# Last four chunks: the second product by seven block products too, with block sums staged in DRAM, seven open accumulators and one bank for the first product

## The chip, the cores and the metric

The kernel runs on one core of one Trainium2 chip. The time is the device time of the whole program in microseconds (us); lower is better. A difference under 2% counts here as no change.

## The reference, cut to what matters

The input is attention without softmax (8 batches, 8 heads, 576 tokens, 64 dims, 128 random features), and its output feeds a feed-forward layer with a squared relu:

```
def phi(x):
    proj = np.einsum('bhsd,df->bhsf', x, w_phi)
    proj = proj - np.max(np.abs(proj), axis=-1, keepdims=True)
    return np.concatenate([np.exp(proj), np.exp(-proj)], axis=-1)
...
num = np.einsum('bhsf,bhfd->bhsd', q_p, kv)
den = np.einsum('bhsf,bhf->bhs', q_p, z)[..., None] + 1e-06
...
h = x @ w_in                 # x is [4608, 512], w_in [512, 2048]
r = np.maximum(h, 0.0)
return (r * r) @ w_out       # w_out is [2048, 512]
```

## The kernel before

**Tiles.** The 4608 tokens of the feed-forward layer are 18 chunks of 256 tokens, d_ff is 8 blocks of 256 columns. One turn is one block of d_ff for one chunk or, late in the program, for a pair of chunks. The first product makes h for the turn in PSUM (the accumulator memory of eight banks), ACT and DVE square it and split it into a high part `gh` (f32r) and a low part `gl` (bf16), and the second product adds the turn's share to an output accumulator that stays open over all 8 turns.

**Precision by passes.** The first product takes each matmul three times in fp16 (high times high, high times low, low times high). The second takes it three times too: bf16 upper part times low weights, bf16 `gl` times rounded weights, and f32r `gh` times high weights. So 12 matmuls of 512 columns make the second product of one chunk and turn (`gemm2`, L1088).

**Chunks 1 to 10 and the pairs.** Ten chunks run with the plain first product (L1051, 24 matmuls of 256 columns) beside the attention work. The last eight chunks run as four pairs: (13,14), (15,16), (17,10), (11,12). After three plain turns at its start, `pair` (L1190) takes the first product of two chunks as one block product of 2 by 2 blocks with seven products instead of eight (L1233): 7 x 6 = 42 matmuls of 256 columns per turn, not 48. They go to three tiles: `pz` (one bank, the first product's a11 b11), `pp` (two banks, four products) and `ph` (one bank, two products). ACT copies `pz` out (L335), DVE adds the blocks together (L1248, three of 512 and one of 256 elements per partition), ACT takes relu and two squares per chunk (L1265, L1068, L1070), DVE makes `gl` (L331). Then comes `gemm2` for each chunk, with accumulators in `po` (two banks) and in `pn` and `pv`. The seven products need sums of blocks of the weights (`add_w`) and of the inputs (`add_x`), made on DVE in the stretch before; the weight sums of all eight blocks of d_ff stay in on-chip memory.

**The order.** One planner (`Plan`) lists every operation with an engine, a duration, what it needs and a rank; `improve` replaces the ranks by those of a written-out table, `RANKS`, for operations whose rank is under `MOVED`, and the resulting list is emitted. Each engine then runs its own list in that order and waits at whatever is not ready: an operation that is late holds back all that stand behind it on its engine.

**The end.** `store` (L1111) scales each finished accumulator of 128 x 512 on ACT (`o`), and a DMA writes it out.

Of the kernel before, what the change touches and what calls it, by code (L numbers as in the profile page):

```python
# [52 lines left out]
MOVED = 70.0  # L53
# [5 lines left out]
PLAIN = 3  # L59
SPILLED = (10, 11, 12)  # L60
# [257 lines left out]
def tile_kernel(ctx, tc, qp, kp, vp, w_phi, w_in, w_out, out):  # L318
# [747 lines left out]

    def squares(n, r, after, use, Q):
        sq = P.add("ACT", act_us(512), lambda: A.activation(out=gh_[n], in_=r(), func=AF.Square),  # L1068
                   after, use + [("gh", n)], Q)
        o = P.add("ACT", act_us(512), lambda: A.activation(out=r(), in_=r(), func=AF.Square),  # L1070
                  [sq], use, Q, other=[("DVE", 0.70, lambda: V.tensor_tensor(
                      out=r(), in0=r(), in1=r(), op=ALU.mult), 4.0)])
        return P.add("DVE", 0.70, lambda: sub(V, gl_[n], r(), gh_[n].bitcast(F32)),
                     [o, sq], use + [("gh", n), ("gl", n)], Q, lock=4.0)
# [51 lines left out]
    def take(use, shape, dtype, box):  # L1126
        if use not in box:
            box[use] = {"e": e_, "qe": qe_, "pt": pt_, "mx": mx_, "n": n_, "rb": rb_, "v": v_, "k": k_, "q": q_, "r": r_}[use[0]].shaped(
                use[1], shape, dtype)
        return box[use]  # L1130

    def combine(fill, sums, use, halves, after, rank):
        one, tm = ("es", NPAIR), lambda: es_[NPAIR]
        o = P.add("DVE", 1.3, fill, after + [ring1] + exps[NPAIR - 2] + in_pair.get("tm", []), [one], rank, lock=4.0)
        o = P.add("DVE", 1.7, sums, [o], [one], rank, lock=4.0)
        hi = P.add("ACT", 1.06, lambda: A.activation(out=halves(0), in_=tm(), func=AF.Copy), [o], [one] + use, rank,
                   other=[("DVE", 0.64, lambda: V.tensor_copy(out=halves(0), in_=tm()), 4.0)])
        o = P.add("DVE", 1.28, lambda: sub(V, halves(1), tm(), halves(0)), [hi], [one] + use, rank, lock=4.0)
        in_pair["tm"] = [o]
        return o  # L1140

    def add_w(f, rank):
        use = {0: [("e", 64)], 1: [("e", 65)], 2: [("e", 66)], 3: [("pt", 32)], 4: [("rb", 32), ("rb", 33)], 5: [("mx", 64), ("n", 32)],
               6: [("qe", 66)], 7: [("v", 36), ("r", PAIRED * NFP + 2 * PLAIN)]}[f]
        box, cs = {}, slice(256 * f, 256 * f + 256)

        def halves(x):
            if len(use) == 2:
                return take(use[x], [128, 1024], F16, box)
            return take(use[0], [128, 2, 1024], F16, box)[:, x, :]  # L1150

        grid = lambda x: x.rearrange("p (h k j c) -> p h k j c", h=2, k=2, j=2)
# [12 lines left out]
        o = combine(fill, sums, use, halves, w_done[f, True], rank)
        parts_w[f] = o, use, lambda x, h, k, j: grid(halves(x))[:, h, k, j, :]

    keep = {}

    def add_x(cs, rows, use, after, rank):  # L1170
# [15 lines left out]

        o = combine(fill, sums, use, halves, [o for c in cs for o in ready(c, (rows, rows + 2))] + after, rank)
        parts_x[cs, rows] = o, use, lambda x, h, i: grid(halves(x))[:, h, i, :]

    def pair(cs, pos, f, turn, po):  # L1190
        n = pos * NFP + 2 * turn
        m = TAIL + n
        Q = m - 1000.0
        g = in_pair["n"] = in_pair.get("n", -1) + 1
        px, py, pu = ("pp", ("w", g)), ("ph", BANKS + PAIRED * NFP + 2 * PLAIN + g), ("pz", ("w", g))
        grid = lambda x: x.rearrange("p (j t) -> p j t", j=2)
        X = lambda i: grid(pp_["w", g][:, i, :])
        Y = lambda: ph_[py[1]]
        rt = ("qe", 64 + g % 2)

        def r():
            if rt not in in_pair:
                in_pair[rt] = qe_.shaped(rt[1], [128, 4, T], F32)
            return in_pair[rt]

        w_ready, w_use, ws = parts_w[f]
        x_ready = [parts_x[cs, i][0] for i in range(2)]
        x_use = [y for i in range(2) for y in parts_x[cs, i][1]]
# [26 lines left out]

        def one():
# [10 lines left out]
        def plus(to, a, b):  # L1247
            V.tensor_tensor(out=to, in0=a, in1=b, op=ALU.add)  # L1248

        wide = lambda x: x.unsqueeze(1).to_broadcast([128, 2, T])  # L1250
        after = list(w_done[f, True]) + [w_ready] + x_ready + in_pair.get("pe", [])
# [4 lines left out]
        p2 = P.add("PE", 2.62, two, [p1], [px, py] + reads, m + 0.01)  # L1256
        in_pair["pe"] = [p2]
# [14 lines left out]
        in_pair["r", g] = done  # L1272

# [55 lines left out]
    free, used = [], []  # L1329
    for k, cs in enumerate(PAIRS):  # L1330
# [8 lines left out]
        for f in range(0 if k else NFP):
            add_w(f, first + 1.5 + f + 1.0 * PLAIN * (f >= NFP - PLAIN))  # L1340
        turns = [*range(NFP - PLAIN, NFP), *range(NFP - PLAIN)] if k == 0 else range(NFP)
        for j, f in enumerate(turns):
            if k or j >= PLAIN:
                pair(cs, v, f, j, po)
            else:
# [4 lines left out]
        free += [(back[c][0] if c in back else SLOT[c], used[-1]) for c in cs]  # L1350
    pool_next.after += pool_prep
# [32 lines left out]
    "L=6CLUTFEO2uPvAD.-.-Ht3`E*LhX{c?L|81TPLM/%B1.CGQn<cD>of`k:Rv35E9p?e$W-WMWIrtOQ1OhEaM9p48lUaroXtSqqwO"  # L1384
    "Qfxx]kEayQn*WdMJ<h=X/Aar|tOBKo0@Nm|e2{=}sZn4q[G={R:AyMy.YirRbF0EF-0jB5/.@uD%JIZbseAlhb.07:d{2-W6Lj=M"
    "IaPC7fA-P|nhy;|gK+UB[M?$mr3#3pJ<Tim?[ygPhFUO^Yz<9]Dq.-dw5k3{m^_H8s23LP@U:S/>N$Dm;#^ZHPVgR+xh_4v(.-ts"
# [55 lines left out]
```

## Time and profile before

| | us |
|---|---|
| runs: 1022.18 and 1020.33, median | 1021.25 |
| span of the profiled execution | 1018.5 |
| PE (TensorE, matmuls) busy | 999.8 (98%) |
| DVE (VectorE) busy | 763.2 (75%) |
| ACT (ScalarE) busy | 680.5 (67%) |
| POOL (GpSimd) busy | 361.2 (35%) |
| granted TensorE clock, mean of the span | 1.00 from 600 us on |

The profiled execution has no other time of its own than its span; the runs' times are device times with the start and end of the program, so the median is 2.75 us above the span. The last 320 us hold the pairs. The columns of each view stand at its first group below. PE rows show a matmul's time from its start to its modelled end, so that consecutive ones overlap: the pace of the engine is the distance of their starts.

### The profile page before, as it was taken

The page shows a single profiled execution, that of the slowest core. Times are in us where ns is not written, and L with a number is a line of the kernel's source. Part 1 is how long each engine was busy: PE and PEld are TensorE (multiplying, and loading weights), DVE is VectorE, ACT ScalarE, POOL GpSimd, SP SyncE. Part 2 cuts the span into 40 slices and gives each one's busy share as a digit, 9 for nine tenths or more (in the row PEclk, how much of TensorE's full clock was granted, in tenths as well). Part 3 has the DMA queues.
Part 4 walks back from the last instruction along what each step waited for, and adds up shares of the span by engine and source line. Part 5 has one row for each costly group of instructions (what it writes and reads, how often), then busy time and mean ns, then how long its engine had stood idle before and what let it go on. Part 6 is the DMA issues. An engine that isn't in the chain of part 4 may idle for free.

```text
span 1018.5 us, 19261 instructions
## 1 busy us (share of the span) xinstructions
PE 999.8 (98%) x7632; PEld 694.6 (68%) x7713; DVE 763.2 (75%) x1221; ACT 680.5 (67%) x1206; POOL 361.2 (35%) x138
## 2 busy tenths in 40 slices
PE   8999999999999999999999999999999999999998
PEld 4657776776666667666767666666776767677675
DVE  5899878798878989777879888798888447343432
ACT  6989886777777787686777867776555445435444
POOL 2433356364456555475375646563000000000000
PEclk9999999999999999999999999999999999999999
DMA  9754323132322233233324212110002001000001
GB/s 355 282 186 135 122 81 94 39 110 73 85 60 81 75 93 93 60 82 81 107 80 111 83 48 69 41 41 22 13 2 83 1 1 49 14 1 21 22 1 42
DMA packets 94914, 77.34 MB, mean 76 GB/s; under 512 B 58088, under 2 KB 72424, under 8 KB 92776
## 3 DMA queue, kind: packets, MB, share of 16 engines
q1 hardware_dynamic: 94536, 75.59, 24.6%
q8 instruction: 60, 0.98, 0.4%
q10 hardware_dynamic: 288, 0.52, 0.1%
q14 instruction: 30, 0.25, 0.1%
HBM read 61.16 MB, written 14.78 MB: 75 GB/s over the span
## 4 chain that ended last, share of the span: by engine, by line
PE 90%; DVE 3%; DMA 3%; ACT 2%; issue 1%; SPq 0%; DVEq 0%; ACTq 0%
PE po L1088 27%; PE ph L1051 21%; PE pp L1233 7%; PE pz L669 4%; PE pv L1088 4%; PE pn L1088 4%; PE ph L1233 3%; PE pn L904 3%; PE pn L884 2%; PE pp L611 2%; PE pv L904 2%; PE pz L1233 2%; PE pz L674 1%; PE pv L669 1%; PE pz L892 1%
## 5 line engine op out<-in xcount | busy, mean ns | idle before, releaser
L1051 PE MATMUL ph<-ring,win 128*128 128x256 f16 x2064 | 240.4, 273 | 0.8 <-ACT r L1060 0.8
L1051 PEld LDWEIGHTS <-win 128*128 128x128 f16 x2064 | 195.3, 98 | 47.0 <-issue 24.8
L982 POOL PARTITION_ALL_REDUCE mx<-pt x52 | 121.6, 2339 | 122.7 <-ACT pt L335 84.3
L1088 PE MATMUL po<-wh,gh 128*128 128x512 f32 x448 | 143.8, 442 | 0.0
L1003 POOL PARTITION_ALL_REDUCE rb<-rb x26 | 96.5, 3712 | 112.0 <-DVE rb L1000 95.6
L1265 ACT ACTIVATE qe<-qe,cw 128x512 f32<-128x512 f32 x58 | 41.4, 715 | 112.5 <-DVE qe L1248 112.5
L1088 PE MATMUL po<-wl,gl 128*128 128x512 bf16 x448 | 115.1, 379 | 0.0
L331 DVE TENSOR_TENSOR gl<-r,gh 128x512 bf16<-128x512 f32 x86 | 87.5, 1018 | 31.7 <-ACT r L1070 30.7
L1003 POOL PARTITION_ALL_REDUCE ds<-ds x26 | 98.7, 3797 | 25.2 <-DVE ds L1000 24.5
L1088 PE MATMUL po<-wl,gh 128*128 128x512 bf16 x375 | 101.5, 379 | 4.9 <-issue 1.6
L1088 PEld LDWEIGHTS <-gl 128*128 128x128 bf16 x576 | 56.4, 98 | 68.0
L1088 PEld LDWEIGHTS po<-wh,gh 128*128 128x128 f32 x448 | 84.6, 189 | 25.9
L1248 DVE TENSOR_TENSOR qe<-pp,qe 128x512 f32<-128x512 f32 (+1 forms) x87 | 52.3, 602 | 61.3 <-PE pp L1233 59.5
L1060 ACT ACTIVATE r<-ph,cw 128x512 f32<-128x512 f32 x86 | 58.7, 683 | 51.0 <-PE ph L1051 49.3
L331 DVE TENSOR_TENSOR gl<-qe,gh 128x512 bf16<-128x512 f32 x58 | 40.1, 691 | 65.7 <-ACT qe L1070 65.6
L1088 PEld LDWEIGHTS <-gh 128*128 128x128 bf16 x576 | 52.3, 98 | 50.7 <-issue 8.9
L633 ACT ACTIVATE e<-e 128x512 f32<-128x512 f32 x64 | 40.0, 625 | 32.3 <-DVE e L630 32.3
L1233 PEld LDWEIGHTS <-win 128*128 128x128 f16 x522 | 48.8, 98 | 14.2 <-issue 7.8
L1068 ACT ACTIVATE gh<-r 128x512 fp32r<-128x512 f32 x86 | 54.1, 629 | 5.7 <-PE pv L1088 2.0
L1070 ACT ACTIVATE r<-r 128x512 f32<-128x512 f32 x86 | 54.3, 631 | 2.7
L650 DVE TENSOR_TENSOR es<-e 128x512 f32<-128x512 f32 x52 | 46.3, 890 | 4.5 <-ACT e L635 4.3
L669 PE MATMUL pz<-e,v 128*64 128x256 f32 x416 | 49.3, 379 | 0.0
(286 smaller groups left out, 1970.4 us busy)
## 6 DMA issues: line engine op xcount, KB each, us to landing
v<-in_vp_dram SPq DMA_DIRECT2D x32, 320.0 KB, 4.1
k<-in_kp_dram SPq DMA_DIRECT2D x32, 288.0 KB, 4.1
q<-in_qp_dram SPq DMA_DIRECT2D x32, 288.0 KB, 3.4
rb<-rd SPq DMA_DIRECT2D x64, 144.0 KB, 3.1
out_dram<-o SPq DMA_DIRECT2D x34, 256.0 KB, 2.1
td<-kvs SPq DMA_DIRECT2D x26, 128.0 KB, 2.6
kz<-td SPq DMA_DIRECT2D x26, 128.0 KB, 2.9
spill<-ring SPq DMA_DIRECT2D x6, 256.0 KB, 2.9
```

Of the source, the lines that this page charges most:

```text
L331: eng.tensor_tensor(out=out_, in0=a, in1=b_, op=ALU.subtract)
L669: PE.matmul(out=to[64 * h:64 * h + 64, 0:256], lhsT=v_[p][:, t, h, :], rhs=e_[2 * p + h][:, t].rearrange("p s f -> p (s f)"), start=t == 0 ...
L904: PE.matmul(out=to[64 * h:64 * h + 64, :], lhsT=kz_[n][:, 128 * s_ + 64 * h:128 * s_ + 64 * h + 64], rhs=qe_[2 * n + h].rearrange("p (s x) ...
L982: o = P.add("POOL", par_us(S), lambda n=n, h=h: G.partition_all_reduce(mx_[n], pt_[p][:, h, :], channels=128, reduce_op=bass_isa.ReduceOp. ...
L1003: o = P.add("POOL", 3.6, lambda y=y: G.partition_all_reduce(y(), y(), channels=128, reduce_op=bass_isa.ReduceOp.add), [o], [home], R(RQ + ...
L1051: PE.matmul(out=ph[:, j, :], lhsT=win[w][:, t, 128 * ff:128 * ff + 128], rhs=at_ring(c, x, t), start=k == 0, stop=k == 3 * KT - 1)
L1060: o = P.add("ACT", act_us(512, 1), lambda: A.activation(out=r_[n], in_=ph_[bank], func=AF.Relu, scale=cw[:, f, 0:1]), [g1], [("ph", bank), ...
L1068: sq = P.add("ACT", act_us(512), lambda: A.activation(out=gh_[n], in_=r(), func=AF.Square), after, use + [("gh", n)], Q)
L1070: o = P.add("ACT", act_us(512), lambda: A.activation(out=r(), in_=r(), func=AF.Square), [sq], use, Q, other=[("DVE", 0.70, lambda: V.tenso ...
L1088: PE.matmul(out=bank(i), lhsT=x[:, j, 128 * i:128 * i + 128], rhs=w[:, j, :], start=turn + j + s == 0, stop=(turn, j, s) == (NFP - 1, 1, 2))
L1233: PE.matmul(out=to, lhsT=fl(x, *al)(k), rhs=fr(y, *ar)(k), start=n == 0, stop=n == 5)
L1248: V.tensor_tensor(out=to, in0=a, in1=b, op=ALU.add)
```

## The change

Constant `FROM` = 2: the pairs 3 and 4 (chunks 17, 10, 11, 12; 16 of the program's turns) go through a new function `blocks`. Pairs 1 and 2 keep `pair`. The first three turns of pair 1 stay plain.

- In `blocks` the first product has the same 42 matmuls, but in four pieces pa, pb, pc, pd (6, 12, 12, 12 matmuls), which all go through the one bank `ph`. Each piece is taken out by ACT (pa) or DVE (pb, pc, pd) before the next may start.
- The second product of a chunk is a product of 2 by 2 blocks too: seven products of 3 matmuls of 256 columns, 42 matmuls per turn for the two chunks instead of 24 of 512 columns. Each of the seven has an accumulator of its own (128 x 256, open over all 8 turns): both chunks' fill the seven other banks.
- New per turn: DVE makes four sums S0 to S3 of the squared blocks (both chunks in one instruction, 256 elements per partition), ACT and DVE split them into `hs` and `ls` (two instructions each, 512 elements).
- New after a pair: `collect` adds the seven accumulators of a chunk together (one ACT copy, DVE o1 to o4), ACT scales four blocks of 128 x 256, and two DMAs write them out.
- Sums of blocks of w_out (`make_t`) are made during pairs 1 and 2, stored to DRAM (1 MB per block of d_ff) and loaded again per turn. The sums of w_in (`make_w`) have two buffers now, are stored when made, and loaded again per turn (512 KB).
- `MOVED` goes from 70 to 1000: the table `RANKS` now sets the order of the whole program, and it has new contents.

```diff
-MOVED = 70.0
+MOVED = 1000.0
+FROM = 2
...
+    def blocks(cs, pos, f, turn, k, w_part, t_part):
...
+        two = lambda i, x, y: lambda: (product(bank(i)[:, 0, :], *x), product(bank(i)[:, 1, :], *y))
...
+        pa = P.add("PE", 0.66, lambda: product(bank(0)[:, 0, :], "a11", "b11"), after, [("ph", i0)] + reads, m)
+        first, other = copy(T, lambda: r()[:, 1, :], lambda: bank(0)[:, 0, :])
+        ca = P.add(*first, [pa] + old, us(0), Q - 300.0, other=[other])
+        pb = P.add("PE", 1.31, two(1, ("a12", "b21"), ("s2", "t2")), [pa], [("ph", i0 + 1)] + reads, m + 0.01)
+        cb_ = P.add("DVE", dve_us(512), lambda: plus(r()[:, 0:4:3, :], bank(1), wide(r()[:, 1, :])), [ca, pb], us(1), Q - 300.0)
+        pc = P.add("PE", 1.31, two(2, ("s3", "t3"), ("s1", "t1")), [pb], [("ph", i0 + 2)] + reads, m + 0.02)
+        cc_ = P.add("DVE", dve_us(512), lambda: plus(r()[:, 1:3, :], bank(2), wide(r()[:, 3, :])), [cb_, pc], us(2), Q - 300.0)
+        c22 = P.add("DVE", dve_us(T), lambda: plus(r()[:, 3, :], bank(2)[:, 0, :], r()[:, 2, :]), [cc_], us(2), Q - 300.0)
+        pd = P.add("PE", 1.31, two(3, ("a22", "t4"), ("s4", "b22")), [pc], [("ph", i0 + 3)] + reads, m + 0.03)
...
+        cd = P.add("DVE", dve_us(512), lambda: plus(r()[:, 1:3, :], bank(3), r()[:, 1:3, :]), [pd, c22], us(3), Q - 300.0)
...
+        for fn in (lambda E: add(E, S(0), a(1, 0), a(1, 1)), lambda E: sub(E, S(1), S(0), a(0, 0)),
+                   lambda E: sub(E, S(2), a(0, 0), a(1, 0)), lambda E: sub(E, S(3), a(0, 1), S(1))):
+            x = [P.add("DVE", dve_us(256), lambda fn=fn: fn(V), x, [rt, st], Q + 0.2, lock=4.0,
+                       other=[("POOL", pool_us(256), lambda fn=fn: fn(G), 0.0)])]
...
+            y = P.add("ACT", out_us(512), lambda hs=hs, i=i: A.activation(out=hs(), in_=s()[:, i], func=AF.Copy), after, [st] + use, Q + 0.3,
+                      other=[("DVE", 0.42, lambda hs=hs, i=i: V.tensor_copy(out=hs(), in_=s()[:, i]), 4.0)])
+            y = P.add("DVE", dve_us(512), lambda hs=hs, ls=ls, i=i: sub(V, ls(), s()[:, i], hs().bitcast(F32)), [y] + reading.get((z, 1), []), [st] + use, Q + 0.3, lock=4.0)
...
+                for s_ in range(3):
+                    for q_n, (bank_n, d), xs, ws in what:
+                        if xs[0] == "a":
+                            x = (upper(buffer(z, 0)), buffer(z, 1), buffer(z, 0))[s_][:, 2 * xs[2] + xs[1], :]
+                        else:
+                            x = (upper(hs()), ls(), hs())[s_][:, xs[1], :]
+                        if ws[0] == "b":
+                            w = (low, near, highs[f])[s_][:, ws[1], 256 * ws[2]:256 * ws[2] + 256]
+                        else:
+                            w = t_at(tb, (1, 2, 0)[s_])[:, ws[1], :]
...
+                        PE.matmul(out=to, lhsT=x, rhs=w, start=not turn and not s_ and begin,
+                                  stop=turn == NFP - 1 and s_ == 2 and q_n in ((1, 3, 5, 6) if i else (3, 5, 6)))
...
+    def collect(c, v, i, banks, Q):
...
+        o0 = P.add(*first, [told[0, 1], told[1, 1]], [rx, ry], Q, other=[other])
+        o1 = P.add("DVE", dve_us(512), lambda: plus(X(), at(0), wide(Y()[:, 0, :])), [o0, told[i, 6]], [rx, ry] + banks, Q)
+        o2 = P.add("DVE", dve_us(512), lambda: plus(Y(), at(1), wide(X()[:, 1, :])), [o1, told[i, 5]], [rx, ry] + banks, Q)
+        o3 = P.add("DVE", dve_us(256), lambda: plus(X()[:, 1, :], at(1)[:, 0, :], Y()[:, 1, :]), [o2], [rx, ry] + banks, Q)
+        o4 = P.add("DVE", dve_us(512), lambda: plus(Y(), at(2), Y()), [o3, told[i, 3]], [rx, ry] + banks, Q)
...
+            w_part = w_flow.load(f, m - 8.0) if f in w_flow.stored else w_flow.make(f, m - 8.0, make_w)
+            if k < FROM:
+                pair(cs, v, f, j, po, w_part)
+                continue
+            blocks(cs, v, f, j, k, w_part, t_flow.load(f, m - 8.0))
```

**What stands where on DVE.** Before, DVE's list for one turn of a pair has six instructions: the blocks of pp, ph and pp added (L1248), then `gl` of each chunk (L331):

```order
L1248 TENSOR_TENSOR qe_8746<-pp_10711,qe_8746 128x512 x2
L1248 TENSOR_TENSOR qe_8746<-ph_10742,qe_8746 128x512
L1248 TENSOR_TENSOR qe_8746<-pp_10711,qe_8746 128x256
L331 TENSOR_TENSOR gl_10805<-qe_8746,gh_10801 128x512
L331 TENSOR_TENSOR gl_10836<-qe_8746,gh_10832 128x512
L1248 TENSOR_TENSOR qe_8829<-pp_10788,qe_8829 128x512 x2
```

In the change, a turn of pairs 3 and 4 (squared blocks in qe_8856, the next turn's first product into qe_8770) has twelve. The tile names are reused buffers: qe_8423 holds S0 to S3, gl_10194 is the second chunk's low part, et_10231 and et_10241 are `ls` of the two chunks:

```order
L1320 TENSOR_TENSOR qe_8770<-ph_10839,qe_8770 128x2x256
L332 TENSOR_TENSOR gl_10194<-qe_8856,gh_10165 128x512
L1170 TENSOR_TENSOR qe_8423<-qe_8856 128x2x128
L332 TENSOR_TENSOR qe_8423<-qe_8423,qe_8856 128x2x128
L1320 TENSOR_TENSOR qe_8770<-ph_10866,qe_8770 128x512
L1320 TENSOR_TENSOR qe_8770<-ph_10866,qe_8770 128x256
L332 TENSOR_TENSOR qe_8423<-qe_8856 128x2x128
L332 TENSOR_TENSOR qe_8423<-qe_8856,qe_8423 128x2x128
L332 TENSOR_TENSOR et_10231<-qe_8423,ds_10227 128x512
L1320 TENSOR_TENSOR qe_8770<-ph_10903,qe_8770 128x512
L332 TENSOR_TENSOR et_10241<-qe_8423,v_10229 128x512
L332 TENSOR_TENSOR gl_10281<-qe_8770,gh_10254 128x512
```

In the order of the code's names these are cb of the next turn, gl of the second chunk, S0, S1, cc and c22 of the next turn, S2, S3, ls of the first chunk, cd of the next turn, ls of the second chunk, and then gl of the next turn's first chunk. The addition that frees the bank after pd (cd) stands behind `ls`.

**ACT in the same turn** has nine instructions: relu, square (`gh`) and square in place for each chunk, between them the copy ca of the next turn's pa (L336), and at the end `hs` of both chunks (L1467):

```order
L1437 ACTIVATE qe_8770<-qe_8770,cw 128x512
L1443 ACTIVATE gh_10254<-qe_8770 128x512
L336 ACTIVATE qe_8856<-ph_10707 128x256
L1445 ACTIVATE qe_8770<-qe_8770 128x512
L1437 ACTIVATE qe_8770<-qe_8770,cw 128x512
L1443 ACTIVATE mx_10283<-qe_8770 128x512
L1445 ACTIVATE qe_8770<-qe_8770 128x512
L1467 ACTIVATE n_10348<-qe_8423 128x512
L1467 ACTIVATE rb_10350<-qe_8423 128x512
```

Before there are seven: the same six and the copy of `pz`; `hs` is new, and the copy has gone between the squares of the first chunk.

**The end of the program on DVE.** Before, DVE's last work is the two `gl` of the last turn; the accumulators go to ACT only. In the change the last ten instructions of DVE are `ls` of both chunks and o1 to o4 of both:

```order
L332 TENSOR_TENSOR kvs_10352<-qe_8423,n_10348 128x512
L332 TENSOR_TENSOR dn_10362<-qe_8423,rb_10350 128x512
L1320 TENSOR_TENSOR r_11900<-pp_10168,r_11901 128x512
L1320 TENSOR_TENSOR r_11901<-pp_10168,r_11900 128x512
L1320 TENSOR_TENSOR r_11900<-pp_10168,r_11901 128x256
L1320 TENSOR_TENSOR r_11901<-pz_10169,r_11901 128x512
L1320 TENSOR_TENSOR r_11953<-po_11169,r_11954 128x512
L1320 TENSOR_TENSOR r_11954<-po_11170,r_11953 128x512
L1320 TENSOR_TENSOR r_11953<-po_11170,r_11954 128x256
L1320 TENSOR_TENSOR r_11954<-pn_10203,r_11954 128x512
```

Each of these four reads what the one before it wrote, and ACT's four scalings of the chunk (L1542) stand behind the last of them.

## Rows read from the trace of the kernel before

**Rows 1.** Page, span and part 1: busy us (share of span), instructions
```profile
span 1018.5 us, 19261 instructions
PE 999.8 (98%) x7632; PEld 694.6 (68%) x7713; DVE 763.2 (75%) x1221; ACT 680.5 (67%) x1206; POOL 361.2 (35%) x138
```
**Rows 2.** Windows of the pairs: busy us and (instructions) per engine, PE clock, DMA
```profile
700.00:800.00 100.00, 97.88 (x651) 69.21 (x658) 84.18 (x132) 53.38 (x82) 4.96 (x2) 1.00 0.08 25
...
900.00:1018.50 118.50, 113.93 (x738) 79.79 (x746) 43.65 (x68) 51.26 (x84) 0.00 (x0) 1.00 0.05 19
```
**Rows 3.** Timeline at PE's two longest late waits: start, us; [idle before <- releaser]
```profile
705.74 0.69 ACT L1060 ACTIVATE r<-ph,cw 128x512 f32<-128x512 f32 x1 [2.21 <-PE ph L1051]
...
706.48 0.70 PE L1051 MATMUL ph<-ring,win 128*128 128x256 f16 x5 [0.78 <-ACT r L1060]
...
781.03 0.83 PE L1233 MATMUL pp<-ring,win 128*128 128x256 f16 x6 [0.87 <-DVE qe L1248]
```
**Rows 4.** Chain that ended last, 850 to 1020: start, us, instructions
```profile
900.47 2.62 PE pp L1233 x24
...
909.74 0.67 PE pz L1233 x6
910.41 2.62 PE pp L1233 x24
913.03 1.31 PE ph L1233 x12
```
**Rows 5.** Timeline of the end: PE, then ACT's last scaling
```profile
1008.96 0.61 PE L1088 MATMUL po<-wl,gh 128*128 128x512 bf16 x2
...
1010.31 0.61 PE L1088 MATMUL po<-wl,gh 128*128 128x512 bf16 x2
...
1013.69 0.82 PE L1088 MATMUL pv<-wh,gh 128*128 128x512 f32 x2
1014.66 0.69 ACT L1111 ACTIVATE o<-pv,cc 128x512 f32<-128x512 f32 x1 [0.64 <-DMA out_dram<-o]
```
**Rows 6.** Lines by form: count | busy us, mean ns of one | idle before
```profile
L1088 PEld LDWEIGHTS po<-wh,gh 128*128 128x128 f32 x448 | 84.6, 189 | 25.9
L1088 PEld LDWEIGHTS <-gl 128*128 128x128 bf16 x576 | 56.4, 98 | 68.0
L331 DVE TENSOR_TENSOR es<-es 128x256 f32<-128x256 f32 x56 | 24.7, 442 | 1.8
L1248 DVE TENSOR_TENSOR qe<-pp,qe 128x256 f32<-128x256 f32 x29 | 12.3, 424 | 1.0
L335 ACT ACTIVATE qe<-pz 128x256 f32<-128x256 f32 x27 | 10.2, 379 | 21.3 <-PE pz L1233 21.3
L1155 DVE TENSOR_TENSOR es<-win,win 128x1024 f32<-128x1024 f16 x8 | 9.7, 1213 | 0.1
```
**Rows 7.** Timelines with f32 weight loads: two of 128 columns, then PE with sixteen
```profile
21.05 0.30 PEld L422 LDWEIGHTS pn<-ident,m 128*128 128x128 f32 x2 [0.24 <-PE pv L714]
...
308.88 1.90 PE L669 MATMUL pz<-e,v 128*64 128x256 f32 x16
310.60 0.60 PE L674 MATMUL pz<-et,v 128*64 128x256 f32 x4
```
**Rows 8.** Timelines of DVE and ACT, one turn of a pair
```profile
962.82 1.42 DVE L1248 TENSOR_TENSOR qe<-pp,qe 128x512 f32<-128x512 f32 x2 [4.02 <-PE pp L1233]
...
965.06 0.72 ACT L1265 ACTIVATE qe<-qe,cw 128x512 f32<-128x512 f32 x1 [4.55 <-DVE qe L1248]
...
966.48 0.63 ACT L1070 ACTIVATE qe<-qe 128x512 f32<-128x512 f32 x1
967.02 0.71 ACT L1265 ACTIVATE qe<-qe,cw 128x512 f32<-128x512 f32 x1
...
968.42 0.63 ACT L1070 ACTIVATE qe<-qe 128x512 f32<-128x512 f32 x1
```
**Rows 9.** Page, part 2: GB/s that the DMA engines moved, in 40 slices
```profile
GB/s 355 282 186 135 122 81 94 39 110 73 85 60 81 75 93 93 60 82 81 107 80 111 83 48 69 41 41 22 13 2 83 1 1 49 14 1 21 22 1 42
```

More of the change, by code (lines that the diff above doesn't have):

```diff
@@ L1127, in take @@
         if use not in box:
-            box[use] = {"e": e_, "qe": qe_, "pt": pt_, "mx": mx_, "n": n_, "rb": rb_, "v": v_, "k": k_, "q": q_, "r": r_}[use[0]].shaped(
+            box[use] = {"e": e_, "qe": qe_, "pt": pt_, "mx": mx_, "n": n_, "rb": rb_, "v": v_, "k": k_, "q": q_, "r": r_,
+                        "ds": ds_, "et": et_, "kz": kz_, "kvs": kvs_, "dn": dn_, "gh": gh_, "gl": gl_}[use[0]].shaped(
                 use[1], shape, dtype)
         return box[use]
[L1132 to L1140, printed above, removed]
@@ new lines, in tile_kernel, with t_at, w_put, w_get @@
+    spare_after = lambda: [o for c in range(NCH) if SLOT[c] in spare_slots for o in chunk_done.get(c, [])]
+    def t_at(b, x):
+        if not x:
+            return take(t_home(b)[0], [128, 4, 256], F32R, keep)
+        half, c0 = place(spare_slots[b % 2])
+        return ring[half][x - 1][:, :, c0:c0 + T].bitcast(BF16)
+    def w_put(f, b):
+        return 1 if f is None else SP.dma_start(ws_[f], w_at(b))
+    def w_get(f, b):
+        return 1 if f is None else SP.dma_start(w_at(b), ws_[f])
@@ L1245, in two @@
             product(Y()[:, 1, :], "s4", "b22")
[L1247 to L1251, printed above, removed]
+        after = list(w_done[f, True]) + w_ready + x_ready + in_pair.get("pe", [])
         if not turn:
@@ L1329, in tile_kernel @@
     free, used = [], []
+    in_pair["ph"] = BANKS + PAIRED * NFP + PLAIN + FROM * NFP
+    in_pair["r_at"] = PAIRED * NFP + 2 * PLAIN
+    taken_over = P.add("PE", 0.0, lambda: None, [], [], TAIL + PAIRED * NFP)
+    late_f = [*range(NFP - PLAIN, NFP)]
+    turns = [late_f + [*range(NFP - PLAIN)]] + [[*range(NFP)]] * 3
+    pool_back = P.add("POOL", 6.2, lambda: None, [op for op in P.ops if op.eng == "POOL" and op.rank > PER_PAIR * EARLY], [], -100.0)
     for k, cs in enumerate(PAIRS):
@@ L1336, in tile_kernel @@
         for i in range(2):
-            add_x(cs, i, homes[k % 2][2 * i:2 * i + 2], used[k - 2] if k > 1 else [], first + 0.5 * i)
+            add_x(cs, i, homes[k % 2][2 * i:2 * i + 2], used[k - 2] if k > 1 else list(t_flow.stored.values()) if FROM < 2 else [], first + 0.5 * i - 6.0 * min(k, 2))
+        if not k:
+            for f in range(NFP):
+                t_flow.stage(f, first + 2.0 + (2.0 * FROM - 1.0) * f, make_t)
         po = [[("po", 2 * BANKS + PAIRED + v + i) for i in range(2)], [("pn", ("o", v // 2)), ("pv", ("o", v // 2))]]
[L1339 to L1345, printed above, removed]
+        in_pair["pool"] = k + 1
+        if k == FROM:
+            in_pair["busy"] = True
+        for j, f in enumerate(turns[k]):
+            m = TAIL + v * NFP + 2 * j
+            if not k and j < PLAIN:
                 for i in range(2):
```

380 lines of the change are left out of this document (309 added, 71 removed).

## The prediction, made before the changed kernel ran

> **What bounds the kernel now.** First the page: TensorE (PE) is busy 999.8 of 1018.5 us; DVE has 25% of its time free, ACT a third [rows 1]. What PE has left is 18.7 us, so a change gains only by shortening PE's own list, and loses wherever it makes PE wait. Second, the windows of the pairs: from 900 us on PE has 113.9 of 118.5 us, the clock is granted in full (1.00), DVE works 43.7 us and ACT 51.3; but in 700:800, where the sums for the pairs are made, DVE is busy 84% [rows 2]. So pairs 3 and 4 have room on DVE and ACT, pair 1 has little. Third, the timeline where PE waits longest late in the program: 0.78 us at 706 for ACT and 0.87 us at 780 for DVE, both for an accumulator to be read out [rows 3]. The first shows what a hand-over costs: ACT's read ends at 705.74 + 0.69 = 706.43, PE starts at 706.48, 0.05 us later. Fourth, the chain of waits in the last pairs: nothing but PE, one turn per 910.41 - 900.47 = 9.94 us, of which the first product takes 0.67 + 2.62 + 1.31 = 4.60 us (24 matmuls of 256 columns in 2.62, so 0.109 each), and the second product the other 5.34 us [rows 4].
>
> All sums below are against the span of 1018.5 us; the median of the runs, 1021.25, is 2.75 us above it, and I add that at the end.
>
> **The change part by part.**
>
> *Fewer columns on PE.* The second product of a turn goes from 24 matmuls of 512 columns to 42 of 256: 48 x 0.109 = 5.23 us becomes 42 x 0.109 = 4.58 us of streaming. The 5.34 measured is 0.11 above its streaming, and the turn has 8 f32 matmuls: 0.014 us for each. At the end six matmuls of 512, two of them f32, take 1010.31 - 1008.96 = 1.35, which is 0.04 above 12 x 0.109: 0.02 for each f32 one [rows 5]. The new list has 14 products of three matmuls, with one f32 each: 3 x 0.109 + 0.02 to 0.03 = 0.35 to 0.36; I take 0.36. Turn: 4.60 + 14 x 0.36 = 9.64, against 9.94. Sixteen turns: **-4.8 us**. The lower bound of a product is 0.327 (no extra), a turn of 9.18, -12.2 us. The upper bound is in the weights: one f32 load shows 189 ns, a 16-bit one 98 [rows 6]; a load of 189 behind a matmul of 109 would add 0.08 per product, 0.44 in all, a turn of 10.76. Against it: two such loads together take 0.30 us, so that the second starts 0.11 after the first, and sixteen f32 matmuls of 256 columns, each with a load, go by in (310.60 - 308.88)/16 = 0.108 each [rows 7]. That is the nearest row and the reason for 0.36.
>
> *The new loop through one bank.* Before, the first product has three tiles and waits for none of them in these turns. Now each piece must be read out of `ph` before the next starts. From the end of a last matmul's stream to the end of its record goes 0.16 us (five matmuls show 0.70, of which 5 x 0.109 stream [rows 3]), and I take the hand-over of 0.05 to the reader and back. With ACT's 379 ns [rows 6] that is 0.64 us after pa; with DVE's 0.69 (two in 1.42 [rows 8]) 0.95 after pb and pd, and with c22's 424 ns [rows 6] behind it 1.4 after pc. The usual order of PE has three, three, five and three products between the pieces (1.08, 1.08, 1.80, 1.08 us), so the bank by itself is covered. What is not is DVE's place: cd, which frees the bank after pd, stands behind `ls`, and `ls` hangs on a loop: cd 0.69; ACT's six instructions 3.99 (965.06 to 968.42 + 0.63 [rows 8]) and the copy ca 0.3 between them; gl 0.69; S0, S1 0.88 (442 ns each [rows 6]); cc and c22 1.11; S2, S3 0.88; hs 0.68; ls 0.69; some 0.15 for the hand-overs. That is 10.1 us. Neighbours that don't depend on each other overlap (ACT's 966.48 + 0.63 ends 0.09 after the next began at 967.02 [rows 8]); four such places on DVE take it to 9.75. I take 9.9: PE waits 0.26 us per turn in the 14 middle turns, **+3.6 us**. Bounds: 0 where the loop is under PE's 9.64, and 0.76 x 14 = 10.6 where DVE or ACT slips to 10.4 (some turns have only one or two products between two pieces, each missing one 0.36).
>
> *Entry.* In the first two turns of pair 3 there are no second products to put between pieces: pa and pb, pd and pa, and again pa and pb stand side by side, 0.64 + 0.95 + 0.64 = 2.2 us. The first S products then need the whole loop once: from cd some 10 us, and PE has 8.3 us of work there: 1.4 more, after overlap. **+3.6 us** (2.2 to 5).
>
> *Pair boundary and end.* Between pairs 3 and 4 `collect` puts 2 x (3 x 0.69 + 0.42) = 5.0 us on DVE, and the new pair's first products wait for the banks it reads; PE has the first product of the new pair meanwhile: **+2.5 us** (1 to 5). In the last turn no first product is left to cover the loop; from the last piece 9 us of cd, ACT, gl, S, hs and ls stand before the last S products, about as long as the products that are left, so I take **+1.2 us** (0 to 3). After the last matmul there was one ACT scaling of 0.69 [rows 5]; now there are what is left of o2, o3, o4 (1.9 us after overlap) and four scalings of 256, about 1.6: **+2.7 us** (2 to 3.7).
>
> *Sums and transfers in pairs 1 and 2.* The sums of w_out cost DVE 1.2 (1213 ns [rows 6]) + 4 x 0.44 + about 1.2 for the low part, 4.2 us each, 34 in all, into 16 turns whose DVE is 84% busy at the start and under half later: **+1 us** (0 to 4). The loads are 1.5 MB per turn, 159 GB/s; the DMA engines moved 355 in the first slice and under 50 in most of the last ten [rows 9], and two buffers give them a turn's lead: 0. They stand on SP's queue, where little else is left but the outputs. If a load were late, PE would stop at the first product that uses it.
>
> *The order of the whole.* In the new order eight other matmuls stand between the two tiles that made PE wait at 706, and ten at 780: **-1.65 us** [rows 3]. The order of the first 600 us changes little; 0.
>
> Sum: -4.8 + 3.6 + 3.6 + 2.5 + 1.2 + 2.7 + 1.0 - 1.65 = +8.15. Span 1026.7, **1029 us** as a median of runs.
>
> **The rivals.**
> - *The loop is covered and products are cheap: faster.* If products take 0.336 (0.009 extra, under the 0.014 of the long ones) a turn is 9.30 and the gain 10.2; with entry 3, middle 1, boundary 1.5, end 0.5 + 2.7, sums 0 and -1.65 the sum is -3.2: 1018; with the middle at 0 and entry 2.2, 1016. It needs DVE's loop to come down by 0.6 us per turn. For it: DVE and ACT are under half busy there [rows 2]. Against it: the loop is a chain, and idle time in it is waiting for its own links. Range 1010 to 1021; chance 0.22.
> - *DVE's list slips: slower, within 2%.* Turn 10.4, +10.6 in place of +3.6: 1036 (1034 to 1041). It decides where the middle turns show PE waiting for cd more than 0.5 us. Chance 0.14.
> - *f32 weights bound the short matmuls: slower.* Each f32 load, now behind a matmul of 256 columns and not of 512, takes its 189 ns: a product 0.44, a turn 10.76, 13.1 us lost in place of 4.8 gained. DVE's loop is then hidden (-3.6 of it): +8.15 + 17.9 - 3.6 = +22.5, 1044. It decides from 0.02 us above the 0.36 of a product (0.38 costs what the columns save). For it: 189 against 98 [rows 6]; against it: the loads 0.11 apart [rows 7]. Chance 0.07.
>
> On this rival, the Trainium skill ("TensorE: Matmul & The Clock Gate", section "Weight-path perf modes — Fast Weight Load (FWL) and DoubleRow") says that the fast load is given to 128 weights of any type but FP32: it speaks against a change that loads f32 weights twice as often per column, and 189 against 98 agrees [rows 6]. The same page's "LDWEIGHTS (loading the stationary operand)" reckons a load by its columns over 1.2, an estimate of 107 ns for 128: by that it just hides behind 109, a turn stays 9.64 and the rival falls; the 0.11 between two loads agrees with this one [rows 7].
>
> **How the numbers follow.** The forecast of 1029 (its own range 1021 to 1036, from the bounds of the loop, the entry and the boundary) has a chance of 0.55; the three rivals 0.22, 0.14 and 0.07; 0.02 is left for what I have not seen. Signs are mixed, so the range takes in most of the faster rival and most of the slip: 1011 to 1040 leaves out a tenth of the forecast and of these two, and the weights. More than 2% (20 us, about what a measurement of this kernel can tell from no change) is 1000.8 or 1041.7: faster could come only from the lower bound of every term, 0.01; slower is the weights and the end of the slip, 0.09; the rest, 0.90, is within.
>
> **What would show it.** In the trace after: the starts of pa in pairs 3 and 4 9.9 us apart, with PE idle 0.2 to 0.4 us a turn before pa, released by DVE's addition from `ph`, and nearly none before pb, pc and pd; three-matmul products 0.36 apart; the last matmul about 4 us before the last scaling ends; no waits of 0.8 us at the start of pair 1. Products of 0.38 or more would make the weights right; a turn under 9.7 without waits the faster rival; idle time before pb or pc a slip. Waits for a DMA on PE, or a granted clock under 1.00, would be neither forecast nor rival.

## The result, and the profile after

The changed kernel takes **1031.88 us** (median of 1030.05 and 1033.7) against 1021.25: a ratio of 1.0103 (95% interval 1.0056 to 1.0151), a small loss, within the 2% taken as no change. The forecast was 1029, range 1011 to 1040. Run again beside the experiments the change took 1033.88 against 1020.57, 1.0124 (1.0099 to 1.0148). One execution of a later run, the profiled one of `square_dve2`, went at a granted clock of 0.655 and took 1469 us; nothing below is read from it.

The profiled execution's span went from 1018.5 to 1031.9 us, by 13.4 us, while the medians are 10.6 apart. The runs on record that have both times take 1.8 us more than their span (1033.7 against 1031.9). So the profiled execution of the change is the slower of its two, that of the kernel before (1018.5, hence 1020.33) the faster, and of the 2.75 us between span and median in the prediction about 1 is scatter. Where the two traces part is read from the first matmul of each stage:

| stage | before | after | difference |
|---|---|---|---|
| to the first product of pair 1 | 722.39 | 726.00 | +3.61 |
| pairs 1 and 2 | 127.57 | 126.79 | -0.78 |
| pair 3 to the last turn of pair 4 | 149.06 | 149.38 | +0.32 |
| last turn to the end of the last matmul | 15.49 | 20.86 | +5.37 |
| from there to the end | 4.02 | 8.89 | +4.87 |

The third and fourth rows do not hold the same work. When the last turn begins, the change still has 36 second products to do, eight more than the 28 of two turns; eight are 2.8 us. For the same work the third row is about +3.2 and the fourth +2.5.

The page after (its span and part 1) and the windows of the pairs; they answer to [rows 1, 2]:

```profile
span 1031.9 us, 20283 instructions
...
PE 1004.3 (97%) x8002; PEld 717.5 (70%) x8002; DVE 823.3 (80%) x1383; ACT 710.8 (69%) x1262; POOL 359.9 (35%) x140
```

```profile
700.00:800.00 100.00, 100.00 (x689) 71.73 (x689) 91.30 (x143) 63.59 (x96) 4.98 (x2) 1.00 0.39 130
...
900.00:1031.90 131.90, 117.52 (x1012) 100.99 (x1009) 87.39 (x163) 70.66 (x128) 0.73 (x1) 0.98 0.47 152
```

DVE is fuller in pair 1 (91%) and PE still has no idle time there: the sums are hidden. From 900 us on DVE's work has doubled and PE leaves 14 us unused, 9 of them at the end; the granted clock of 0.98 is theirs too (0.73 from 1024 to 1031, where no matmul runs). PE's busy time is no measure of the columns saved: the page before lacks some matmul records (7632 of 7713 loads), this one none.

PE's waits (engine, line, releaser: us in all, times, longest):

```profile
PE ph L1314 <- DVE qe L1320: 3.8, 7, 0.9
...
PE ph L1314 <- ACT qe L336: 1.4, 3, 0.5
...
PE pp L1489 <- DVE r L1320: 0.8, 1, 0.8
...
PE pp L1489 <- DVE et L332: 0.6, 1, 0.6
...
PE pz L1489 <- DMA e<-ws: 0.3, 1, 0.3
```

The one bank's hand-overs lead (ph): all ten stand at the entry of pair 3, at the boundary of the pairs and in the last three turns. The last row names a load, but that matmul, at 867.50, reads `gl`, which DVE had finished at 867.44 (its row: start 866.75, 0.69 us). So none of the new loads is shown to make PE wait. These rows hold only what PE's modelled ends don't cover. A middle turn shows more. The chain of waits through one, from pc (898.02) to pa (903.76):

```profile
898.02 1.34 PE ph L1314 x12
...
899.39 0.70 DVE qe L1320
...
900.11 0.42 DVE qe L1320
...
900.54 0.68 DVE qe L332 x2
...
901.24 0.64 ACT n L1467
...
901.90 0.70 DVE kvs L332
...
902.65 1.11 PE pp L1489 x8
903.76 0.67 PE ph L1314 x6
```

pc, then cc, c22, S2 and S3, `hs`, `ls`, and then eight matmuls of the products behind pd. On PE's timeline the same place:

```profile
902.27 0.27 PE L1489 MATMUL pp<-ring,n 128*128 128x256 bf16 x1
902.65 0.28 PE L1489 MATMUL pp<-ring,kvs 128*128 128x256 bf16 x1
902.69 0.36 PE L1489 MATMUL pp<-pt,n 128*128 128x256 f32 x1
...
903.61 0.83 PE L1314 MATMUL ph<-ring,win 128*128 128x256 f16 x6
```

The product's second matmul takes `ls` (kvs) and starts 0.38 us after the first, not 0.11: a wait of 0.27 us inside the product, of which the bars leave only 0.11 open, since the first bar lasts 0.27. So in this loop I took waits as the distance of starts less the matmuls' own time. That gives 4.2 us at the entry of pair 3, 1.3 in the middle turns, 2.4 at the boundary of the pairs, 1.8 before two pieces of the last three turns and 2.3 behind the last piece. Products themselves take 0.355 us, and a turn without waits 9.55 (turn 4 of pair 3).

The 1.3 us of the middle turns are three waits of 0.28 for `ls` (turns 5, 7 and 8 of pair 3) and two of 0.24 and 0.25 for the bank (turn 6 of pair 3, turn 1 of pair 4), where only two products stand between pb and pc. The turns 4, 5 and 7 of pair 4 have no wait at all. There PE's list runs the second products three to six products (1.1 to 2.1 us) further behind the pieces of the first product than in pair 3, so that `ls` is in time; that this is the reason is argued from the lists, and no run tests it.

Two of the bank's waits, at the entry and at the boundary, then two waits of the last turn, for the bank and for `ls` (et):

```profile
854.09 0.82 PE L1314 MATMUL ph<-ring,win 128*128 128x256 f16 x6 [0.47 <-ACT qe L336]
...
952.02 0.81 PE L1314 MATMUL ph<-ring,win 128*128 128x256 f16 x6 [0.89 <-DVE qe L1320]
...
1009.35 0.50 PE L1314 MATMUL ph<-k,win 128*128 128x256 f16 x3 [0.91 <-DVE qe L1320]
...
1012.22 0.28 PE L1489 MATMUL pp<-ring,et 128*128 128x256 bf16 x1 [0.57 <-DVE et L332]
```

And the end, which answers to [rows 5]; the last matmul ends at 1023.03:

```profile
1020.76 0.27 PE L1489 MATMUL pp<-ring,n 128*128 128x256 bf16 x1 [0.78 <-DVE r L1320]
...
1023.27 1.30 ACT L1542 ACTIVATE o<-r,cc 128x256 f32<-128x256 f32 x3 [2.02 <-DVE r L1320]
...
1024.48 0.36 ACT L336 ACTIVATE r<-pv 128x256 f32<-128x256 f32 x1
1024.88 1.94 DVE L1320 TENSOR_TENSOR r<-po,r 128x512 f32<-128x512 f32 x3 [1.64 <-ACT r L336]
...
1026.86 0.69 DVE L1320 TENSOR_TENSOR r<-pn,r 128x512 f32<-128x512 f32 x1
1027.58 1.30 ACT L1542 ACTIVATE o<-r,cc 128x256 f32<-128x256 f32 x3 [1.15 <-DVE r L1320]
```

Chunk 12's collection starts with the copy at 1024.48, 1.5 us after its last matmul: until then ACT scales chunk 11 out of the two r buffers that the copy needs. The whole chain o1 to o4 then runs bare, and the last scaling ends at 1028.88, 5.85 us after the last matmul, where about 4 were forecast.

### The profile page after: what moved, and what is told of

Read it like the earlier page. It is cut to its first block, busy times and chain, and to the rows that moved or that the text cites. A ratio compares the mean times of both kernels' runs of the same rounds, so it can differ in the third digit from the quotient of the medians.

```text
span 1031.9 us, 20283 instructions
## 1 busy us (share of the span) xinstructions
PE 1004.3 (97%) x8002; PEld 717.5 (70%) x8002; DVE 823.3 (80%) x1383; ACT 710.8 (69%) x1262; POOL 359.9 (35%) x140
## 4 chain that ended last, share of the span: by engine, by line
PE 85%; DVE 6%; ACT 5%; DMA 2%; issue 1%; SPq 0%; ACTq 0%; DVEq 0%
PE po L1092 24%; PE ph L1052 22%; PE ph L1314 7%; PE pz L670 4%; PE pp L1314 3%; PE pn L905 3%; PE pn L885 3%; PE pv L905 2%; PE pp L612 2%; PE pn L1092 2%; PE pv L1092 2%; PE pp L1489 2%; DMA v<-in_vp_dram 2%; DVE qe L1320 2%; PE po L1489 1%
## 5 line engine op out<-in xcount | busy, mean ns | idle before, releaser
L1092 PE MATMUL po<-wh,gh 128*128 128x512 f32 x384 | 122.9, 441 | 0.0
L332 DVE TENSOR_TENSOR gl<-r,gh 128x512 bf16<-128x512 f32 x86 | 78.6, 913 | 34.7 <-ACT r L1073 34.4
L1092 PE MATMUL po<-wl,gl 128*128 128x512 bf16 x384 | 98.6, 379 | 0.8 <-DVE gl L332 0.8
L1092 PEld LDWEIGHTS po<-wh,gh 128*128 128x128 f32 x384 | 72.5, 189 | 22.1
L1092 PEld LDWEIGHTS <-gl 128*128 128x128 bf16 x448 | 43.7, 98 | 53.9 <-DVE gl L332 1.3
L1314 PEld LDWEIGHTS <-e 128*128 128x128 f16 x696 | 66.8, 98 | 10.0 <-issue 1.9
L1092 PEld LDWEIGHTS <-gh 128*128 128x128 bf16 x448 | 41.5, 98 | 37.0 <-issue 8.2
L1320 DVE TENSOR_TENSOR qe<-ph,qe 128x512 f32<-128x512 f32 x77 | 48.9, 635 | 20.2 <-PE ph L1314 17.1
L628 DVE TENSOR_REDUCE km<-pp 128x4 f32<-128x512 f32 x54 | 36.2, 681 | 33.7 <-PE pp L612 33.7
L332 DVE TENSOR_TENSOR qe<-pt,mx 128x576 f32<-128x576 f32 x52 | 43.6, 838 | 9.1 <-POOL mx L983 8.8
```

The source lines that it names most:

```text
L332: eng.tensor_tensor(out=out_, in0=a, in1=b_, op=ALU.subtract)
L1092: PE.matmul(out=bank(i), lhsT=x[:, j, 128 * i:128 * i + 128], rhs=w[:, j, :], start=turn + j + s == 0, stop=(turn, j, s) == (NFP - 1, 1, 2))
L1314: PE.matmul(out=to, lhsT=fl(x, *al)(k), rhs=fr(y, *ar)(k), start=n == 0, stop=n == 5)
```

## The experiments

**1. The early order.** `early_old` gives the first 1108 operations the old ranks in the changed kernel, `before_newearly` the new ones in the kernel before (the tables are put in words here):

```diff
-RANKS = (new table, 2738 operations)
+RANKS = (old entries for the 1108 ranks under 70, new for the rest)
```

> The changed kernel with the old table of ranks for the 1108 operations of the attention and the ten plain chunks; the pairs keep the new ranks. Theory (the new order of the first 130 us costs PE about 3.5 us): the first product of pair 1 starts near 722.4 us as before the change and not at 726.0, and the median falls from 1031.9 to about 1028.4. Rival (the 3.6 us are the scatter of one execution, or come from extra work in that stretch): the first product of pair 1 stays near 726 and the median near 1031.

> The kernel before with the new table's ranks for the same 1108 operations and nothing else of the change. Theory (new early order costs 3.5 us): the median rises from 1021.3 to about 1024.8, the first product of pair 1 at 726 us, and the single waits of 0.2 us per 50 us after 100 us are fewer. Rival (scatter): 1021, with pair 1 at 722.

Measured: 1087.83 (ratio 1.066) and 1085.61 (1.0644), with the first product of pair 1 at 779.8 and 775.1 us, and PE idle for some 40 us between 100 us and there. Both miss what was expected, by some 60 us. The likely reason, not tested, is that the planner interleaves what it is given, so that ranks fitted to one program order another one badly. They tell nothing of the question. So I fixed the emitted order instead. Up to about 308 us both kernels run the same set of operations:

```diff
+        put = {n: i for i, n in enumerate(FIRST)}    # order of the other kernel
...
-        for _, _, fn in sorted([(op.start, op.n, op.fn) for op in order] + fills, ...):
+        for _, _, fn in sorted([(put[op.n], op.n, op.fn) if op.n in put else (1e6 + op.start, op.n, op.fn) ...
```

> The changed kernel, but its first 1148 operations (what either kernel does up to about 308 us, the same set in both) are emitted in the order of the kernel before, with that kernel's filling matmuls; everything behind stays in the new order. Theory (the new order of the first 100 us costs 3.5 us, most of it between 70 and 90 us): the first product of pair 1 starts at 722 to 723 us and the median falls by 3 to 4 us against the changed kernel. Rival (the loss is scatter or comes later): 726 and the same median.

> The kernel before, but its first 1154 operations (to about 311 us) in the new order of the changed kernel, with that kernel's filling matmuls. Theory (the new order of the first 100 us costs 3.5 to 5 us, whatever follows): the first product of pair 1 starts near 726 in place of 722.4 us, and the median rises from 1020.5 to 1024 to 1025.5. Rival (the loss comes from something else that the changed kernel does early, such as its pools and homes): 722 and 1020.5.

> The changed kernel once more, unchanged, as the base of the runs beside it. Expected: a median of 1030 to 1032, the first product of pair 1 at 726 us, middle turns of 9.8 us.

`early_cut`: 1031.48 beside 1033.88 for the change in the same job, pair 1 at 721.7 (after_again 726.8). The median falls by 2.4 us and not by 3 to 4, and the single runs of the two overlap (1029.51 to 1033.43, 1032.1 to 1035.66). `before_newcut`: 1025.95 against 1020.28, ratio 1.0053 (1.0037 to 1.0069), pair 1 at 728.2. In both pair 1 follows the order, not the kernel. Over these traces the new early order reaches pair 1 at 722.7 to 728.2 (eight, mean 726.3), the old one at 721.7 to 723.0 (three, 722.4): about 4 us, with a wide scatter, part of which goes with the granted clock (last section). In the two traces compared above 2.3 of the 3.6 us are lost between 70 and 90 us; PE's busy time there in the kernel before, the change and `early_cut`:

```profile
70.00:90.00 20.00, 19.64 (x209) 13.51 (x209) 18.43 (x31) 19.18 (x31) 3.98 (x3) 1.00 0.48 156
```

```profile
70.00:90.00 20.00, 17.32 (x186) 11.17 (x182) 18.56 (x33) 17.96 (x29) 1.76 (x2) 1.00 0.30 87
```

```profile
70.00:90.00 20.00, 19.04 (x199) 12.88 (x200) 17.30 (x27) 17.39 (x27) 5.91 (x4) 1.00 0.45 154
```

**2. What the middle turns wait for.** `no_sums` left out the operations before planning; `no_sums2` keeps every list and leaves out the instructions alone:

```diff
+        made = told["made"] = told.get("made", -1) + 1
...
-            x = [P.add("DVE", dve_us(256), lambda fn=fn: fn(V), x, ...
+            x = [P.add("DVE", dve_us(256), lambda fn=fn, made=made: fn(V) if made < 2 else None, x, ...
```

> The changed kernel, with S0 to S3, hs and ls computed in the first two turns of pair 3 only; later turns leave them out and multiply the old ones, so PE's matmuls and the loads stay. Theory (the middle turns wait for a loop over DVE and ACT of which S, hs and ls are 3.1 us): the middle turn falls from 9.83 us to PE's own 9.55 to 9.62, the waits of the last turn (2.7 us) mostly go, the median falls by 5 to 7 us to about 1026. Rival (the middle turn is PE's own time, with f32 weights or changes of type dearer than 0.36 a product): the turn stays at 9.75 or more and the median falls by 2 to 3 us only, in the last turn.

> The changed kernel, every list in its own order, with S0 to S3, hs and ls issued in the first two turns of pair 3 only; later turns leave these instructions out and multiply the old sums, so PE's list is the same instruction for instruction. Theory (the middle turns wait for the loop over DVE and ACT): the middle turn falls from 9.8 to PE's own 9.55 to 9.65, the waits of the last turn mostly go, the median falls by 4 to 7 us. Rival (the middle turn is PE's own time): the turn stays at 9.75 or more, the median falls by 1 to 3 us, in the last turn.

`no_sums` was planned into another order (1051.36, turns of 11 to 12 us) and is of no use. `no_sums2`: 1032.87, 1.0 under after_again, which is within the scatter of the runs; so it is read by its turns. Three of the four turns of 9.83 to 9.86 fall to 9.55 (the first waits for sums that are still made); those with only two products between pb and pc stay at 9.78, with 0.24 us for the bank. So the sums are what those three turns wait for, but it is 0.8 us in all. The last turn, up to the last matmul, gains 1.0 more (19.85 against 20.86 us). The rest of the expected gain was not there: the last turn's waits of 1.05 us before pd, for the bank, and for o1 stayed.

`third_bf16` prices the f32 pass and speeds PE up against the loop:

```diff
-                            x = (upper(buffer(z, 0)), buffer(z, 1), buffer(z, 0))[s_][:, 2 * xs[2] + xs[1], :]
+                            x = (upper(buffer(z, 0)), buffer(z, 1), upper(buffer(z, 0)))[s_][:, 2 * xs[2] + xs[1], :]
```

(and likewise for `hs`, `near` in place of the high weights.)

> The changed kernel with the third pass of every product of the new second product in bf16 (both operands) in place of f32r; the rest, orders and loads included, is the same. It leaves out the f32 pass, so it tells what f32 weights and the change of type cost in a product. PE alone would save 14 x 0.028 = 0.4 us per turn. Theory (the loop over DVE and ACT sets the middle turn): the turn stays at 9.6 to 9.8 us, the wait moves to PE's idle time, the median falls by 1 to 3 us. Rival (PE's own time sets it): the turn falls to 9.4 us, the median by 6 us.

The median is 1030.9 us. A product takes 0.327, the f32 pass therefore costs 0.028 us of it. PE's own turn would be 9.17; the middle turns of pair 3 take 9.54 to 9.59 (one 9.37), and now the chain runs from turn to turn:

```profile
913.65 0.70 DVE qe L1320
...
914.38 0.73 ACT qe L1437
...
918.52 0.69 DVE kz L332
...
920.00 0.66 DVE qe L1320
...
922.48 0.70 DVE kvs L332
...
923.23 0.72 PE pp L1489 x5
```

From cd (913.65) to the product behind the next pd (923.23): 9.58 us. The loop of the prediction exists, but it is 9.58 long and not 9.9. PE's own turn of 9.55 covers it in the change to within 0.03 us, so the waits of 0.28 must come from something else: the theory is the shorter chain from pc. Two tests of that:

```diff
+            ... A.activation(out=half_r(), in_=half_r(), func=AF.Square) if i else V.tensor_tensor(out=half_r(), in0=half_r(), in1=half_r(), op=ALU.mult),
```

> The changed kernel, every list in its order, with one instruction per turn moved from ACT to DVE: the square in place of the first chunk (128 x 512), so that ACT's part of the loop is 0.6 us shorter and DVE's work per turn 0.7 us longer. Theory (PE waits before pa because cd stands behind ls, at the end of a chain through ACT): the waits of 0.26 to 0.29 us before pa in turns 3, 5, 7 and 8 of pair 3 go, these turns fall from 9.8 to 9.55 us, and the wait of 1.05 us in the last turn shrinks; 1 to 2 us in all, median 1032 to 1033 beside 1033.9. Rival (DVE's list is too full, its instructions late): the turns stay at 9.8 or grow, the median rises.

No gain: ratio 1.0135 (1.0111 to 1.0158). Its turns are read from `combo2` below, which has the same edit: 9.82 to 9.86 us, with waits of 0.27 to 0.32 where the change has 0.24 to 0.28. Making ACT's part 0.6 us shorter and DVE's 0.7 longer doesn't help, so the waits don't hang on ACT alone; a chain through both engines the run can't exclude.

```diff
+        s1, s2 = P.ops[n + 1], P.ops[n + 2]
+        if s1.start < cc_next.start < s2.start:
+            s2.start = cc_next.start - 1e-4
```

> The changed kernel with one instruction of DVE moved ahead of cc and c22 in seven turns: S2 (128 x 256, 0.42 us). PE's and ACT's lists and the work are the same. Theory (the wait before pa ends a chain that starts anew in each turn with the piece pc: cc, c22, S2, S3, hs, ls, cd, and then pa, against PE's 15 + 12 + 9 matmuls, and no loop from turn to turn): DVE stood idle 0.17 us before cc, so S2 costs cc little, the chain is about 0.3 us shorter, and the waits of 0.26 to 0.29 us before pa in turns 4, 6, 8 of pair 3 and 1 of pair 4 fall under 0.1, these turns from 9.8 to 9.55; the median falls by about 1 us, less than the scatter. Rival (a closed loop over DVE and ACT, in which the same instructions stand in another order): the waits stay at 0.2 to 0.3.

Three waits of 0.28 fall under 0.1, and their turns of 9.83 to between 9.54 and 9.63; the first, 0.3 in turn 3, stays. The median, 1032.28, says nothing at this size. The three products behind pd, in the chain of `s2_first`:

```profile
899.20 1.13 PE pp L1492 x9
900.32 0.67 PE ph L1314 x6
```

Nine matmuls in 1.13 us, where the change took 1.34 (902.27 to 903.61). So these waits end a chain that starts anew with each pc; it is no loop.

**3. The end.** `tail` moves chunk 12's collection to free memory:

```diff
+            X = lambda: w_at(last_slot ^ 1)[:, 0, :].bitcast(F32).rearrange("p (j t) -> p j t", j=2)
...
-        o1 = P.add("DVE", ..., [o0, told[i, 6]], ...
+        o1 = P.add("DVE", ..., [o0, told[i, 6]] + ([told[i, 5]] if v - i == NCH - 2 else []), ...
...
+                need = [o1, o3, o4] if not last else [{(0, 0): o1, (1, 1): o3}.get((t, d), o4)]
```

> The changed kernel with another end: chunk 12's collection in the free memory of the w_in sums (instead of the two r buffers that chunk 11's scalings hold), its outputs there too; o1 of chunk 11 only after product 5; each scaling waits only for the sum that it reads, and one of the last goes to DVE. Theory (buffers and order at the end cost 2.5 to 3 us): PE's wait of 0.78 us near 1020 is gone, the stretch from the last matmul to the end falls from 8.9 to about 6.5 us, the median from 1031.9 to about 1029. Rival (the end is set by DVE's chain of o1 to o4 and the output transfers as they are): 8.5 us or more, no change of the median beyond 0.5.

The median is 1031.47 us. The wait of 0.78 is gone, and the stretch from the start of the last turn to the end falls from 29.75 to 27.85 us, 1.9 of the 2.5 to 3 expected. From the last matmul it is 7.9, not 6.5:

```profile
1022.62 1.93 DVE L1320 TENSOR_TENSOR e<-po,e 128x512 f32<-128x512 f32 x3
...
1024.59 0.69 DVE L1320 TENSOR_TENSOR e<-pn,e 128x512 f32<-128x512 f32 x1
1025.31 0.51 ACT L1551 ACTIVATE e<-e,cc 128x256 f32<-128x256 f32 x1 [0.22 <-DVE e L1320]
...
1025.85 0.81 SPq L1559 DMA_DIRECT2D out_dram<-e  x2
```

The copy no longer waits, but DVE still has chunk 11's chain before chunk 12's. The last scaling ends 4.05 us after the last matmul (5.85 in the change), but both outputs leave at once, and the span ends 3.85 us after that scaling where it was 3.04.

**4. All together.** `combo2` has the old early order, the square on DVE, the end of `tail`, and a last turn of pair 4 with a plain second product into the accumulators that belong to one block each (the fourth block in `ph`).

> The changed kernel with the old order of the first 308 us, the first chunk's square on DVE, the last turn of pair 4 with a plain second product (48 matmuls of 256 columns, no sums), and the collection of the last chunk in free memory with its two output transfers on two queues. Theory (each term is where the traces put it): early -5, square -1.5, last turn and tail -3 to -4, so 1033.9 falls to about 1024, still 3 to 4 us above the kernel before, because the entry (4 us), the boundary of the pairs (2.4) and the collections stay. Rival (the terms overlap or come back as other waits): 1028 or more.

The median is 1025.78 us, ratio 1.0059 (1.0042 to 1.0076): still behind the kernel before. Its stages: pair 1 at 723.0 us; last turn to the last matmul 19.9 us (20.9); from there to the end 5.3 us (8.9). The square gave nothing. No version here beats the kernel before: the waits at entry and boundary (5.9 us in this trace) are still in it. These two were read from traces alone; no run was aimed at them.

## Why the prediction came out right, step by step

Its number held (1029 forecast, 1031.88 measured), in part by luck: errors of both signs cancelled, and two terms, the last turn and the tail, came out above their own bounds (3 and 3.7). Terms against the span, forecast and found; the found ones add up to the 13.4 us between the two spans:

| step | forecast | found |
|---|---|---|
| fewer columns | -4.8 | -6.2 |
| middle turns | +3.6 | +1.3 |
| entry | +3.6 | +4.2 |
| boundary of the pairs | +2.5 | +2.4 |
| last turn | +1.2 | +4.0 |
| tail | +2.7 | +4.9 |
| sums, and the wait at 780 (pairs 1 and 2) | +0.1 | -0.8 |
| order before pair 1, with the wait at 706 | -0.8 | +3.6 |

None of the rivals came as a whole. No product took 0.38, and the middle turns of pair 3 lie between 9.55 and 9.86 us. In pair 4 the starts of pa are 9.2 to 10.5 apart, because its turns hold 8 to 16 products each. The signs are mixed: turns under 9.7 without waits, the sign of the faster rival, are there (turn 4 of pair 3), and that rival's 1 us for the middle turns was nearer than my 3.6; two waits before pc, a sign of the slip, are there too. The sign forecast for my own account, PE idle before pa in each turn for DVE's addition from `ph`, is not: before pa only the entry and the boundary show it.

Columns: a product is 0.355 us, a turn without waits 9.55, and 16 of them save 6.2 against 9.94. The f32 pass costs 0.028 us of a product (`third_bf16`). The Trainium skill ("TensorE: Matmul & The Clock Gate", section "LDWEIGHTS (loading the stationary operand)") reckons a load by its columns over 1.2, an estimate of 107 ns for 128; the 0.355 agrees with it, while the 189 ns of the record would have shown as 0.44.

Middle turns: the wait was forecast before pa, released by the addition from `ph`, in 14 turns. It is inside the first product behind pd, released by `ls`, and in three turns. `ls` was the right instruction; the step that failed is the length of the loop, 9.58 us (`third_bf16`) and not 9.75 to 10.1, so that PE's own turn covers it.

Entry: right in place and size: 0.64, 0.96, 0.63 were forecast as 0.64, 0.95, 0.64, and the rest of the entry takes 1.9 us where 1.4 was forecast. Boundary: right in size, by luck. I forecast waits for the banks that `collect` reads; no row shows one. All 2.4 us are hand-overs of `ph`: 0.34, 0.34 and 1.06 where two, three and no products stand between the pieces, and 0.63 for ACT's copy of pa, which came late.

Last turn: under-sized by 2.8. I reckoned one chain as long as the products left, but waits come one after another: 0.71 and 1.06 us for the bank, where two products and one stand behind pc against the 1.4 us of cc and c22, and then 0.74, 0.61 and 0.94 for `et`, `kvs` and o1.

Tail: under-sized by 2.2. I took 1.9 us of chunk 12's chain as left after the last matmul; the whole of it is, 2.7 us, and it starts 1.9 us late. The r buffers are a part of that: without them (`tail`) it starts 0.85 us after the last matmul, behind chunk 11's chain on DVE. `tail` took 1.0 us of this term back, and 0.9 of the last turn's (the wait for o1).

The order before pair 1: "the order of the first 600 us changes little; 0" is wrong. Pair 1 starts about 4 us later, as two runs that swap the order alone show, `before_newcut` beyond the scatter of its runs; what the clock has to do with it stands in the last section. The wait at 706 went, but one of 0.78 for the same ACT instruction (relu out of `ph`) has come at 567.

## What to carry to other kernels

A block product that saves 0.39 us per turn pays only if its turns outlast its entry, its boundaries and its end: here these cost 15.5 us and 16 turns gave 6.2. Where a table orders the whole program anew, compare the two traces from their first microsecond, even if the change is at the end. And look for waits in the distance of starts: a pipelined matmul's bar hides up to 0.16 us behind its own end.

## What the runs showed that was not expected

In the first 100 us a long PE wait is in some traces followed by a granted clock of 0.83 over 10 us: in the kernel before a wait of 2.3 us at 7.8 and 0.83 in the stretch of 10 to 20 us, in the change one of 1.7 at 20.9 and 0.83 in 20 to 30. In after_again and `early_cut` the stretch of 20 to 30 us reads:

```profile
20.00:30.00 10.00, 7.39 (x89) 4.61 (x90) 3.96 (x12) 5.96 (x13) 4.35 (x4) 0.83 1.02 421
```

```profile
20.00:30.00 10.00, 9.18 (x119) 6.19 (x120) 7.12 (x19) 9.63 (x18) 4.99 (x4) 1.00 1.02 419
```

Such a dip is worth up to 1.7 us, an estimate (0.17 of 10 us). The kernel before and the change have one each, so it explains nothing of their 3.6 us; after_again has one and `early_cut` none, so it can be 1.7 of their 5.1. Compared at the same clock, two answers stand side by side. `s2_first`, with the change's early order and no dip, reached pair 1 at 722.7, while `early_cut` and `combo2`, with the old order and no dip, did at 721.7 and 723.0: no difference beyond the scatter. With one dip the new order is 3.3 to 5.8 us later than the kernel before (five traces, 725.7 to 728.2 against 722.4). So the early order's cost comes and goes with what happens in its first 100 us; how much of it is the clock and how much the waits there, the runs don't tell.
